# Last expert's first product with the slots held in the array and 256 weight columns streamed; layer 1's first expert picked by an early count; zero stores moved beside that expert

## The chip, the core and the metric

The kernel runs on one core of a Trainium2 chip. Time is device microseconds (us) of one execution; the figure that counts is the median of several. The core has a matrix engine (PE in the profile, its weight loads PEld), a vector engine (DVE), a scalar engine (ACT), GpSimd (POOL) and SP, which here only issues DMAs. Each of them runs its own instructions in order.

## What is computed

Retention attention over 2 batches of 8 heads, 768 positions and width 64, then two mixture-of-experts layers with 8 experts each: 1,536 tokens of 512 numbers, hidden width 1,024, one expert for each token. Layer 2 keeps at most 384 tokens for an expert.

```python
def _moe_ref(x, w_gate, w1, w2):
    logits = x @ w_gate
    expert_idx = np.argmax(logits, axis=1)
    ...
    gate_w = probs[np.arange(N), expert_idx]
    for e in range(E):
        mask = expert_idx == e
        xe = x[mask]
        h = np.maximum(xe @ w1[e], 0.0)
        ye = h @ w2[e]
        out[mask] = gate_w[mask, None] * ye

def reference(**kwargs):
    attn_out = _attn_ref(**attn_kwargs)
    x = attn_out.transpose(0, 2, 1, 3).reshape(B * S, H * D)
    x = _moe_ref(x=x, **moe_kwargs)
    return _moe2_ref(x=x, **moe2_kwargs)
```

With the inputs of the runs layer 1's experts get 183, 196, 188, 167, 213, 180, 203 and 206 tokens, in the order of their numbers (counted with the reference).

## The kernel before

**Attention** goes over 12 tiles of 128 tokens (the loop over `n`); each finished tile is stored to `x1d` in main memory by a DMA that ACT issues (`a_store`, L560), and routed: `batch` does that for several tiles at once (`BATCHES`: tiles 0 to 4, then 5 to 7), `route_tile` for the last four. In a batch, `pick` finds each token's expert, `count` (L593) adds tile by tile to the running counts `run`, `rank` and `slots` give each token its place, `place` (L619) makes the table of which token sits in which slot.

**Layers.** An expert has a fixed number of slots, `CAPS`: in layer 1 (`li == 0`) 220 for the first and 236, 220, 208, 200, 192, 184, 176 for the others, which follow by falling count (`finish_route` sorts them). Layer 1's first expert is always expert 0, so its weights are known from the start (`know(0, 0)`). Layer 2's first one is chosen while layer 1 still runs (`choose`, from the counts so far).

**The first expert** begins early. `early` gathers its first 128 slots from the first eight tiles (`eig`), and its first products run in full fp32 on whole weights (`products`, L429, two records for each product) while routing ends. The rest of its slots are gathered once all tiles are stored (`take` in `layer`, index `ig`, L344 on POOL), transposed in `first_x` (L370) and multiplied in the same way. `held` makes the first weight load of the next expert wait for that gather.

**The other experts** split every fp32 weight piece (512 KB, eight for each expert: four of the first product, then four of the second) into a high part by an ACT cast (`whi`, L163) and a low part by a subtraction (`wlo`, L174, on DVE, some on POOL). Weights are stationary and the slots move: high weights by high and low slots in one matmul (L788 or L814), low weights by high slots in a second (L789 or L815). SP loads pieces into four staging buffers `st` (L142), each free again when its `wlo` is done. `between(j, i)` stands after each eighth of expert `j` and issues the loads, splits, transposes and routing that run beside the products; `run_pend` does the same with what the expert before has left.

**Layer 2's last expert** has 128 slots. Its hidden part runs as for the others (`hidden_group`: 32 pairs of 256 and 128 moving columns, halves summed by ACT and DVE); its output part keeps the slots stationary and streams weights in two halves of 256 columns (`o_part`, L829 to L831), each scaled and scattered as soon as it is done.

**Zeros.** `x2d`, layer 1's output in main memory, is filled with zeros by 12 stores that SP issues behind the attention (L700), before layer 1 scatters its rows into it on POOL (`scatter`, L318).

Of the kernel before, what the change touches and what calls it, by code (L numbers as in the profile page):

```python
# [18 lines left out]
P = 128  # L19
# [8 lines left out]
CAPS = ((220, 236, 220, 208, 200, 192, 184, 176), (256, 256, 232, 208, 184, 168, 160, 128))  # L28
# [5 lines left out]
BATCHES = ((0, 5), (5, 8))  # L34
# [11 lines left out]
def _consts(capacity):  # L46
# [21 lines left out]
    put("first", np.broadcast_to(np.array([1e6] + [(E - e) / 16 for e in range(1, E)]), (P, E)))  # L68
# [5 lines left out]
    put("floor", np.broadcast_to(np.array([P] + [0] * (E - 1)), (P, E)))  # L74
# [7 lines left out]
def fused(ctx, tc, qT, kT, vkr, wg, w11, w12, w21, w22, cst, out, capacity):  # L82
# [41 lines left out]

    know(0, 0)
# [123 lines left out]
    def finish_route(rt, li, mix=()):  # L249
# [16 lines left out]
        V.tensor_add(key, nt, rt.get("first", con("first")))  # L266
# [96 lines left out]
    def first_x(rows):  # L363

        cnt = rows.shape[0]
        x = rp.tile([P, KD, P], F32, tag="x0", name="x0", bufs=2)[:, :, :cnt]
        for ks in range(0, 2), range(2, 4):
            tp = mmtile("tp").rearrange("p (k c) -> p k c", k=KD)[:, 0:2, :cnt]
            for i, k in enumerate(ks):
                T.transpose(tp[:, i, :], rows[:, k * P:(k + 1) * P], ident[:cnt, :cnt])  # L370
            A.copy(x[:, ks[0]:ks[-1] + 1], tp)
        return x


    def choose(rin, li):

        nt = mmtile("ch")[:, 0:E]
        T.matmul(nt, ones16, rin["S"], start=True, stop=True)
# [17 lines left out]
    def of_first(rin, a, dt, name):  # L396

        if "one" not in rin:
            return a[:, 0:1]
        junk = rp.tile([P, E], F32, tag="of", name="oj")  # L400
        f = rp.tile([P, 1], F32, tag="rmk", name="of")
        V.scalar_tensor_tensor(junk, a, 1.0, rin["one"], ALU.mult, ALU.mult, accum_out=f)
        if dt == F32:
            return f
        i = cp.tile([P, 1], dt, name=name)
        V.tensor_copy(i, f)
        return i

    def early(rin, xd, n):
# [4 lines left out]
        V.tensor_tensor(most, nt, rin.get("floor", con("floor")), ALU.max)  # L414
# [52 lines left out]
    with tc.tile_pool(name="ap", bufs=3) as ap:  # L467
# [180 lines left out]
        for n in range(NT):  # L648
            a_scores(n)
# [5 lines left out]
            if n:  # L655
                a_past(n - 1)
            if n == first + 2:
                many[0][2]()
            if n == second + 1:
                many[1][2]()  # L660
                many[1][3](3)
# [3 lines left out]
            if n == first + 1:  # L665
                many[0][1]()
            if n == first + 2:
                many[0][3](2)
            if n == first + 3:
                many[0][3](3)  # L670
# [28 lines left out]
        for t in range(NT):  # L699
            nc.sync.dma_start(x2d[t * P:(t + 1) * P, :], zero)  # L700
# [101 lines left out]

    def w2of(q0, f):
# [45 lines left out]
    def layer(li, xd, rin):  # L849
# [16 lines left out]
        def second():  # L866
            x[0] = first_x(rows[0][1])
            go(1)
# [30 lines left out]
        def between(j, i):  # L899
# [3 lines left out]
            if j + 2 == E and li == 0:  # L903
                if i == 0:
                    chosen.append(choose(rt[1], 1))
# [27 lines left out]

        for j in range(E):
# [6 lines left out]
            for i in range(4):  # L941
                if j == 0:
# [8 lines left out]
                    if i == 3:  # L951
                        between(0, i)
                else:
# [90 lines left out]
            elif j + 1 == E and cap == P:  # L1044
# [3 lines left out]
                for i2, lo in enumerate((0, D // 2)):  # L1048
                    p = mmtile("o")[:, 0:D // 2]
                    for i in range(4):  # L1050
                        o_part(q0, cap, h, [p], (2 * i, 2 * i + 1), 0, slice(lo, lo + D // 2))
                        if lo == 0:
                            between(j, 4 + i)
                    ob = xp.tile([P, D], F32, tag="ob", name="ob", bufs=2)[:, 0:D // 2]
                    A.activation(ob, p, AF.Copy, scale=gt[0])
# [315 lines left out]
```

## Time and profile before

| | |
|---|---|
| runs | 441.76, 442.85, 446.30 us; median 442.85 |
| profiled execution | 443.88 us; span of its instructions 442.1 us |
| granted PE clock, mean | 0.983 of full speed |
| busy | PE 411.3 us (93%), DVE 325.3 (74%), ACT 239.2 (54%), POOL 127.0 (29%) |
| DMA | 100.50 MB, mean 227 GB/s |

The span begins with the first instruction and ends with the last; 1.8 us of the execution lie outside. A "row" of the trace is a group of like instructions one behind the other: start, length, engine, line, operation, output and inputs, sizes, how many, and in brackets how long the engine sat idle before it and what ended that. Lengths of matmuls overlap, so the time that one takes of the engine is read from start to start.

### The profile page before, as it was taken

How to read it: one execution, taken by the hardware profiler on the slowest of the kernel's cores; microseconds unless marked ns; L12 is line 12 of the kernel's file. 1: busy time of each engine (PE TensorE's matmuls, PEld its weight loads, DVE VectorE, ACT ScalarE, POOL GpSimd, SP SyncE). 2: the span in 40 equal slices, each digit the busy share in tenths (PEclk: the TensorE clock that was granted, in tenths of full speed). 3: DMA queues.
4: the chain of work that ended last, by engine and by line, in shares of the span. 5: the costliest groups of instructions: out<-in, count | busy, mean ns of one | idle time of the engine just before them, and what ended most of it. 6: DMA issues, size and time to landing. Idle time of an engine off the chain costs nothing.

```text
span 442.1 us, 9412 instructions
## 1 busy us (share of the span) xinstructions
PE 411.3 (93%) x3373; PEld 384.4 (87%) x3373; DVE 325.3 (74%) x858; ACT 239.2 (54%) x493; POOL 127.0 (29%) x102
## 2 busy tenths in 40 slices
PE   8999884998999999999999999998999999999980
PEld 7887674998899999999989898997888999999970
DVE  3658896177989898989899877187586877887830
ACT  2111240266757666667666651366676777878730
POOL 2443113033353535344442204003202303201020
PEclk9999999799999999999999999999999999999996
DMA  8998994628575766666665733559758677777510
GB/s 317 391 310 300 380 387 148 215 97 264 189 257 169 240 212 241 215 234 220 231 218 191 266 128 89 231 191 313 271 184 269 221 261 249 256 245 247 188 43 14
DMA packets 32854, 100.50 MB, mean 227 GB/s; under 512 B 5008, under 2 KB 5520, under 8 KB 32800
## 3 DMA queue, kind: packets, MB, share of 16 engines
q1 hardware_dynamic: 25488, 82.75, 54.1%
q0 software_dynamic: 5008, 13.06, 8.8%
q10 hardware_dynamic: 2304, 4.02, 2.4%
q8 instruction: 28, 0.46, 0.4%
q14 instruction: 26, 0.21, 0.2%
HBM read 87.08 MB, written 13.05 MB: 226 GB/s over the span
## 4 chain that ended last, share of the span: by engine, by line
PE 59%; DVE 16%; DMA 10%; issue 9%; ACT 2%; POOL 1%; POOLq 0%; SPq 0%; ACTq 0%; DVEq 0%
PE y L814 14%; PE h L788 13%; PE y L815 6%; PE h L789 6%; DVE wlo L174 5%; PE h L429 4%; PE cb L1277 4%; DMA vk<-vkr 2%; DMA whole<-w 2%; DVE hs L774 2%; PE tp L359 2%; DVE h L800 2%; DMA rows<-x1d,eig 2%; DVE rkey L209 2%; PE o L829 1%
## 5 line engine op out<-in xcount | busy, mean ns | idle before, releaser
L174 DVE TENSOR_TENSOR wlo<-st,whi 128x1024 fp32r<-128x1024 f32 x107 | 141.2, 1328 | 0.9 <-ACT whi L163 0.9
L163 ACT CAST whi<-st 128x1024 fp32r<-128x1024 f32 x120 | 124.8, 1045 | 25.4 <-DMA st<-w 24.5
L788 PE MATMUL h<-x,whi 128*128 128x416 f32 (+10 forms) x416 | 123.5, 364 | 0.0
L814 PE MATMUL y<-h,whi 128*128 128x416 f32 (+8 forms) x384 | 117.6, 370 | 0.0
L789 PE MATMUL h<-x,wlo 128*128 128x208 f32 (+10 forms) x416 | 104.5, 251 | 0.0
L815 PE MATMUL y<-h,wlo 128*128 128x208 f32 (+8 forms) x384 | 97.3, 253 | 0.0
L788 PEld LDWEIGHTS h<-x,whi 128*128 128x128 f32 x416 | 78.1, 188 | 2.5 <-issue 0.4
L789 PEld LDWEIGHTS h<-x,wlo 128*128 128x128 f32 x416 | 79.5, 191 | 0.1
L814 PEld LDWEIGHTS y<-h,whi 128*128 128x128 f32 x384 | 72.1, 188 | 2.4 <-issue 0.2
L815 PEld LDWEIGHTS y<-h,wlo 128*128 128x128 f32 x384 | 73.4, 191 | 0.0
L174 POOL TENSOR_TENSOR wlo<-st,whi 128x1024 fp32r<-128x1024 f32 x13 | 34.9, 2684 | 57.7 <-ACT whi L163 51.3
L318 POOL DMA_INDIRECT out<-ob,is x14 | 13.9, 995 | 114.8 <-ACT ob L835 111.1
L800 DVE SCALAR_TENSOR_TENSOR h<-hs,h 128x416 fp32r<-128x416 f32 (+10 forms) x52 | 29.0, 558 | 20.7 <-ACT h L799 17.9
L799 ACT ACTIVATE h<-hs 128x416 fp32r<-128x416 f32 (+10 forms) x52 | 27.1, 521 | 31.1 <-DVE hs L774 30.5
L774 DVE TENSOR_TENSOR hs<-h,hb 128x208 f32<-128x208 f32 (+10 forms) x104 | 32.0, 347 | 6.5 <-ACT hb L773 4.8
L429 PE MATMUL h<-x,whole 128*128 128x128 f32 (+1 forms) x256 | 32.4, 288 | 0.0
L318 POOL DMA_INDIRECT x2d<-row,is x16 | 16.5, 1031 | 55.3 <-ACT row L1290 27.6
L429 PEld LDWEIGHTS h<-x,whole 128*128 128x128 f32 x256 | 31.3, 202 | 0.4 <-issue 0.2
L773 ACT COPY hb<-h 128x208 f32<-128x208 f32 (+10 forms) x104 | 28.8, 316 | 4.0 <-PE h L789 2.2
L1288 ACT COPY row<-cb 128x512 f32<-128x512 f32 x11 | 6.4, 585 | 38.9 <-DVE lgb L1283 29.2
L774 DVE TENSOR_TENSOR yt<-y,yb 128x220 f32<-128x220 f32 (+8 forms) x48 | 15.1, 355 | 14.7 <-ACT yb L773 14.7
L829 PE MATMUL o<-whi,h 128*128 128x512 f32 (+1 forms) x64 | 24.3, 380 | 0.0
(185 smaller groups left out, 604.8 us busy)
## 6 DMA issues: line engine op xcount, KB each, us to landing
st<-w SPq DMA_DIRECT2D x120, 512.0 KB, 4.2
vk<-vkr SPq DMA_DIRECT2D x11, 512.0 KB
whole<-w SPq DMA_DIRECT2D x8, 512.0 KB, 8.4
x2d<-zero SPq DMA_DIRECT2D x12, 260.0 KB, 5.8
qb<-qT SPq DMA_DIRECT2D x12, 256.0 KB, 6.8
x1d<-row ACTq DMA_DIRECT2D x11, 260.0 KB, 4.5
kt<-kT SPq DMA_DIRECT2D x11, 256.0 KB, 5.3
vk<-vkr ACTq DMA_DIRECT2D x1, 512.0 KB
```

Of the source, the lines that this page charges most:

```text
L163: A.copy(hi, st)
L174: (eng or V).tensor_sub(lo, st, hi)
L318: ins = nc.gpsimd.indirect_dma_start(dst.rearrange("n (i d) -> (n i) d", i=parts) if parts > 1 else dst[:, :], bass.IndirectOffsetOnAxis(a ...
L429: T.matmul(ps[:, j], w[:, k, j % 2 * P:(j % 2 + 1) * P], x[:, k], start=k == 0, stop=k == KD - 1, skip_group_check=True)
L773: A.copy(b, ps[:, 1, :])
L774: V.tensor_add(out, ps[:, 0, :], b)
L788: T.matmul(ps, hi[:, k, fs], x[:, k, :, :cap], start=k == 0, stop=False, skip_group_check=True)
L789: T.matmul(ps[:, 0, :], lo[:, k, fs], x[:, k, 0, :cap], start=False, stop=k == KD - 1, skip_group_check=True)
L800: V.scalar_tensor_tensor(h[:, sl, 1, :cap], s, 0.0, h[:, sl, 0, :cap], ALU.max, ALU.subtract)
L814: T.matmul(ps[i], hi[:, ds], h[:, f, :, :cap], start=f == 0, stop=False, skip_group_check=True)
L815: T.matmul(ps[i][:, 0, :], lo[:, ds], h[:, f, 0, :cap], start=False, stop=f == KF - 1, skip_group_check=True)
L829: T.matmul(p, h[:, f, 0, ts_], hi, start=f == 0, stop=False)
```

## The change

Four things are changed.

- Layer 1's first expert is no longer expert 0 but the one with the most tokens in the first four tiles. For that the batches become tiles 0 to 3 and 4 to 7 and their steps come about a tile earlier; `choose` is called at tile 7, and `know_first` reads the number on SP before the first weight loads at tile 8. `early` and the gather of the rest pick the chosen expert's column with `of_first` in place of column 0.
- `CAPS` of layer 1 become 240 for the first and 220, 208, 200, 192, 188, 184, 176.
- The 12 zero stores go from behind the attention into `between(0, i)` of layer 1, one or two for each `i`. `first_x` of layer 1's second gather gets 24 small matmuls on ones ahead of its transposes.
- In layer 2's last expert `hidden_rows` keeps the slots stationary and streams 256 weight columns; the result is rectified on ACT, turned by four transposes at a time and split again (`back_hidden`). The first four eighths of the output part are done for both halves ahead of the last four.

```diff
-CAPS = ((220, 236, 220, 208, 200, 192, 184, 176), (256, 256, 232, 208, 184, 168, 160, 128))
+CAPS = ((240, 220, 208, 200, 192, 188, 184, 176), (256, 256, 232, 208, 184, 168, 160, 128))
...
-BATCHES = ((0, 5), (5, 8))
+BATCHES = ((0, 4), (4, 8))
...
-    know(0, 0)
...
-        V.tensor_add(key, nt, rt.get("first", con("first")))
+        V.tensor_add(key, nt, rt["first"])
...
-    def first_x(rows):
+    def first_x(rows, warm=0):
...
-            tp = mmtile("tp").rearrange("p (k c) -> p k c", k=KD)[:, 0:2, :cnt]
+            tp = mmtile("tp")
+            for _ in range(0 if ks[0] else warm):
+                T.matmul(tp[:, 0:P], ones16, ones16, start=True, stop=True)
+            tp = tp.rearrange("p (k c) -> p k c", k=KD)[:, 0:2, :cnt]
...
         for n in range(NT):
+            if n == first + 1:
+                many[0][1]()
             a_scores(n)
...
+            if n == first + 1:
+                many[0][2]()
             if n == first + 2:
-                many[0][2]()
+                know_first = choose(rt1, 0, run[:, BATCHES[0][1], :])
             if n == second + 1:
                 many[1][2]()
-                many[1][3](3)
+                many[1][3](4)
...
             if n == NT - 4:
+                know_first()
                 refill(2)
...
-        for t in range(NT):
-            nc.sync.dma_start(x2d[t * P:(t + 1) * P, :], zero)
...
+    def hidden_rows(q0, x, i, ps):
+
+        hi, lo = (t.rearrange("p (k f) -> p k f", k=KD) for t in wq[q0 + i])
+        o = ps[:, i % 2 * 2 * P:(i % 2 + 1) * 2 * P]
+        for k in range(KD):
+            T.matmul(o, x[:, k, 0, :P], hi[:, k, :], start=k == 0, stop=False, skip_group_check=True)
+            T.matmul(o, x[:, k, 0, :P], lo[:, k, :], start=False, stop=False, skip_group_check=True)
+            T.matmul(o, x[:, k, 1, :P], hi[:, k, :], start=False, stop=k == KD - 1, skip_group_check=True)
+
+    def back_hidden(hr, h, b):
+
+        tp = mmtile("th").rearrange("p (f c) -> p f c", f=4)
+        for f in range(4):
+            T.transpose(tp[:, f, :], hr[:, f * P:(f + 1) * P], ident)
+        sl = slice(4 * b, 4 * b + 4)
+        A.copy(h[:, sl, 0, :P], tp)
+        V.tensor_sub(h[:, sl, 1, :P], tp, h[:, sl, 0, :P])
...
-            x[0] = first_x(rows[0][1])
+            x[0] = first_x(rows[0][1], 24)
...
             refill()
+            if li == 0 and j == 0:
+                for t in range(NT * i // 8, NT * (i + 1) // 8):
+                    nc.sync.dma_start(x2d[t * P:(t + 1) * P, :], zero)
...
+                elif rows_first(j):
+                    if i % 2 == 0:
+                        ps = mmtile("hr")
+                    hidden_rows(q0, x[j], i, ps)
+                    run_pend()
+                    if i == 2:
+                        back_hidden(hr, h, 0)
+                    if i % 2:
+                        hr = xp.tile([P, 2, C0], F32, tag="hs", name="hr", bufs=2).rearrange("p a c -> p (a c)")
+                        A.activation(hr, ps, AF.Relu)
+                    between(j, i)
...
+                some(0, (0, 1))
+                back_hidden(hr, h, 1)
+                some(0, (2, 3))
+                some(1, range(4))
+                for i in range(4):
+                    between(j, 4 + i)
+                for i2 in range(2):
+                    some(i2, range(4, KF))
```

SP, from the last weight loads of the attention on, before (`order_1179` is the sorted list of experts that SP reads a number from, `whole` the first expert's weights, `st` a staged piece):

```order
L142 DMA st<-w 128x1024 x2
L154 DMA whole<-w 128x1024 x4
L142 DMA st<-w 128x1024 x2
L700 DMA x2d<-zero 128x520 x12
L283 TENSOR_LOAD order_1179
L283 ISA x2
L902 TENSOR_LOAD order_1179
L902 ISA x2
L142 ISA
L142 DMA st<-w 128x1024
```

And after, from that reading of the list on (`order_1204`):

```order
L917 TENSOR_LOAD order_1204
L917 ISA x2
L138 ISA
L138 DMA st<-w 128x1024
L138 ISA
L138 DMA st<-w 128x1024
L926 DMA x2d<-zero 128x520
L138 ISA
L138 DMA st<-w 128x1024
L138 ISA
L138 DMA st<-w 128x1024
L926 DMA x2d<-zero 128x520 x5
```

The twelve stores have left the place behind the attention; the first stands behind two loads of layer 1's second expert, five more behind the next two, and the last six, not shown, one or two at a time between the eight loads that follow.

DVE, in the attention at tile 7, before (`run` are the counts, `Am` and `xt` belong to the attention itself):

```order
L506 TENSOR_TENSOR Am<-sc,cs 128x4x128 x2
L1283 TENSOR_REDUCE lgb<-cb 128x8
L523 TENSOR_TENSOR wn_626<-du,wm_489 128x256
L593 TENSOR_TENSOR run<-run,boh 128x8 x5
L553 TENSOR_TENSOR xt<-ot,cs 128x256 x2
L506 TENSOR_TENSOR Am<-sc,cs 128x4x128 x2
```

And after, at the same tile (`ck` to `floor` are `choose`; `bR` are the slots of a tile's tokens):

```order
L504 TENSOR_TENSOR Am<-sc,cs 128x4x128 x2
L1323 TENSOR_REDUCE lgb<-cb 128x8
L380 TENSOR_TENSOR ck<-ch,cs 128x8
L382 TENSOR_REDUCE cm<-ck 128x1
L384 TENSOR_SCALAR one_638<-ck,cm 128x8
L387 SCALAR_TENSOR_TENSOR cj,ce<-one_638,cs 128x8
L389 CAST chosen_643<-ce 128x1
L391 SCALAR_TENSOR_TENSOR first_645<-one_638,cs 128x8
L393 TENSOR_SCALAR floor_647<-one_638 128x8
L521 TENSOR_TENSOR wn_658<-du,wm_489 128x256
L609 TENSOR_SCALAR bR<-iota_79,r_123 128x256 x2
L551 TENSOR_TENSOR xt<-ot,cs 128x256 x2
```

Counts stood there before; now seven operations of `choose` and two of `slots` stand ahead of the tile's `xt`.

PE, at the end of the hidden part of layer 2's last expert and the start of its output part, before:

```order
L788 MATMUL h<-x,whi 128x256
L789 MATMUL h<-x,wlo 128x128
L829 MATMUL o<-whi,h 128x256
L830 MATMUL o<-wlo,h 128x256
L831 MATMUL o<-whi,h 128x256
```

And after (`hr` are the hidden rows, slot by slot, `th` their transposes):

```order
L805 MATMUL hr<-whi,x 128x256
L806 MATMUL hr<-wlo,x 128x256
L807 MATMUL hr<-whi,x 128x256
L844 MATMUL o<-whi,h 128x256
L845 MATMUL o<-wlo,h 128x256
L846 MATMUL o<-whi,h 128x256
L844 MATMUL o<-whi,h 128x256
L845 MATMUL o<-wlo,h 128x256
L846 MATMUL o<-whi,h 128x256
L813 MATMUL th<-cs,hr 128x128 x4
L844 MATMUL o<-whi,h 128x256
```

Three products of 256 weight columns stand where two of 256 and 128 slot columns stood, and the second set of transposes stands behind six products of the output part.

## Rows read from the trace of the kernel before

**Rows 1.** Page, chain that ended last, shares of the span by engine.
```profile
PE 59%; DVE 16%; DMA 10%; issue 9%; ACT 2%; POOL 1%; POOLq 0%; SPq 0%; ACTq 0%; DVEq 0%
```

**Rows 2.** Windows, one expert each: bounds, length, busy time by engine, clock, DMA.
```profile
98.90:125.40 26.50, 24.73 (x163) 22.23 (x162) 23.09 (x57) 17.06 (x34) 11.73 (x7) 1.00 0.65 214
125.40:148.50 23.10, 23.10 (x163) 22.01 (x162) 20.77 (x53) 15.65 (x32) 10.13 (x7) 1.00 0.65 221
148.50:171.00 22.50, 22.50 (x162) 21.94 (x161) 20.15 (x52) 15.36 (x32) 10.09 (x7) 1.00 0.67 225
171.00:193.60 22.60, 22.24 (x162) 21.61 (x161) 20.30 (x55) 15.19 (x32) 10.28 (x7) 1.00 0.65 224
193.60:215.80 22.20, 21.83 (x163) 21.22 (x162) 19.94 (x54) 15.02 (x32) 10.20 (x7) 1.00 0.67 226
215.80:239.20 23.40, 22.35 (x164) 21.09 (x163) 21.02 (x64) 14.87 (x32) 9.30 (x6) 1.00 0.61 213
...
338.10:358.40 20.30, 20.30 (x137) 19.89 (x136) 14.38 (x25) 13.95 (x29) 6.85 (x6) 1.00 0.75 244
...
396.90:414.70 17.80, 17.80 (x142) 17.77 (x141) 14.97 (x30) 13.43 (x31) 1.96 (x2) 1.00 0.73 247
```

**Rows 3.** Timeline of PE, the transposes of layer 1's second gather.
```profile
77.47 0.84 PE L370 MATMUL tp<-cs,rows 92*128 92x92 f32 x4 [5.79 <-DMA rows<-x1d,ig]
```

**Rows 4.** Timeline of POOL, that gather's issue.
```profile
72.13 1.25 POOL L344 DMA_INDIRECT rows<-x1d,ig  x1 [15.64 <-DVE z L303]
```

**Rows 5.** Zero stores, 40 to 90 us: instructions, first and last start, landing times.
```profile
L700 SPq DMA_DIRECT2D x2d<-zero x12: 319/320/745, 52.5 to 66.5; - x12
...
DMA to landing us min/median/max: 5.3/5.8/7.0
```

**Rows 6.** Tile stores to x1d, 40 to 90 us: instructions, first and last start.
```profile
L560 ACTq DMA_DIRECT2D x1d<-row x7: 326/327/345, 41.2 to 66.1; - x7
```

**Rows 7.** Tile stores to x1d, 0 to 40 us: landing times.
```profile
DMA to landing us min/median/max: 3.6/4.2/5.4
```

**Rows 8.** Windows of 2 us around that wait, columns as in rows 2.
```profile
74.00:76.00 2.00, 0.00 (x0) 0.00 (x0) 0.79 (x1) 0.00 (x0) 1.70 (x2) 0.82 0.28 65
...
80.00:82.00 2.00, 2.00 (x12) 2.00 (x10) 0.69 (x1) 0.60 (x1) 0.00 (x0) 0.50 0.83 250
...
84.00:86.00 2.00, 2.00 (x20) 2.00 (x20) 0.67 (x3) 0.64 (x2) 0.00 (x0) 1.00 0.66 264
```

**Rows 9.** Window, products L429 of 128 slots alone (PE, PEld, clock, DMA).
```profile
67.00:71.80 4.80, 4.68 (x41) 4.49 (x40) 1.00 0.60 201
```

**Rows 10.** Windows of the attention at tiles 6 and 10, columns as in rows 2.
```profile
28.35:32.65 4.30, 4.30 (x74) 3.70 (x72) 2.56 (x8) 0.68 (x2) 1.65 (x3) 1.00 0.85 258
...
47.56:53.46 5.90, 4.43 (x67) 3.66 (x65) 5.33 (x20) 1.28 (x2) 1.04 (x1) 1.00 1.01 389
```

**Rows 11.** Timeline of DVE, counting of a batch.
```profile
37.16 1.38 DVE L593 TENSOR_TENSOR run<-run,boh 128x8 f16<-128x8 f16 x5
```

**Rows 12.** Timeline of PE in layer 2's last expert.
```profile
418.81 0.60 PE L1040 MATMUL o<-cs,yt 128*32 128x128 f32 x4
419.16 0.36 PE L788 MATMUL h<-x,whi 128*128 128x256 f32 x1
...
422.90 0.33 PE L829 MATMUL o<-whi,h 128*128 128x256 f32 x1
423.08 0.28 PE L830 MATMUL o<-wlo,h 128*128 128x256 f32 x1
...
425.08 0.36 PE L829 MATMUL o<-whi,h 128*128 128x256 f32 x1
```

**Rows 13.** Timeline of ACT, a cast that waits for its piece.
```profile
99.74 1.06 ACT L163 CAST whi<-st 128x1024 fp32r<-128x1024 f32 x1 [1.74 <-DMA st<-w]
```

**Rows 14.** Loads of weight pieces, 93 to 108 us: instructions, first and last start.
```profile
L142 SPq DMA_DIRECT2D st<-w x6: 333/333/642, 93.8 to 104.7; - x6
```

**Rows 15.** Timeline of DVE, the index of layer 1's second gather.
```profile
67.12 0.17 DVE L242 TENSOR_TENSOR ig<-tbp,tb 128x16 int32<-128x16 f32 x1 [0.53 <-PE cnt L245]
```

More of the change, by code (lines that the diff above doesn't have):

```diff
@@ L67, in _consts @@
     put("tok", P * np.arange(NT)[None, :] + s[:, None])
-    put("first", np.broadcast_to(np.array([1e6] + [(E - e) / 16 for e in range(1, E)]), (P, E)))
     put("tie", np.broadcast_to((E - np.arange(E)) / 16, (P, E)))
@@ L73, in _consts @@
     put("held", np.broadcast_to(np.array(CAPS[1]), (P, E)))
-    put("floor", np.broadcast_to(np.array([P] + [0] * (E - 1)), (P, E)))
     cand = np.arange(P) // NM
@@ L372, in first_x, with choose @@
         return x
-    def choose(rin, li):
+    def choose(rin, li, S):
         nt = mmtile("ch")[:, 0:E]
-        T.matmul(nt, ones16, rin["S"], start=True, stop=True)
+        T.matmul(nt, ones16, S, start=True, stop=True)
         key = rp.tile([P, E], F32, tag="ju", name="ck")
@@ L396, in of_first @@
     def of_first(rin, a, dt, name):
-        if "one" not in rin:
-            return a[:, 0:1]
         junk = rp.tile([P, E], F32, tag="of", name="oj")
@@ L413, in early @@
         most = rp.tile([P, E], F32, tag="ju", name="most")
-        V.tensor_tensor(most, nt, rin.get("floor", con("floor")), ALU.max)
+        V.tensor_tensor(most, nt, rin["floor"], ALU.max)
         V.tensor_scalar(rin["S"], most, ident[:, 0:1], None, ALU.mult)
@@ L664, in fused @@
                 many[0][0]()
-            if n == first + 1:
-                many[0][1]()
-            if n == first + 2:
+            if first < n < first + 3:
                 many[0][3](2)
-            if n == first + 3:
-                many[0][3](3)
             if n == second:
@@ L904, in between @@
                 if i == 0:
-                    chosen.append(choose(rt[1], 1))
+                    chosen.append(choose(rt[1], 1, rt[1]["S"]))
                 if i == 2:
@@ L932, in between, with rows_first @@
                 gate[j + 1] = gate[j + 1][1]()
+        def rows_first(j):
+            return li == 1 and j + 1 == E and caps[j] == P
         for j in range(E):
@@ L1047, in layer, with some @@
                     V.tensor_scalar(ix2[:, i:i + 1], ix["isc"][:, j:j + 1], 2.0, float(i), ALU.mult, ALU.add)
[L1048 to L1053, printed above, removed]
+                ps = [mmtile("o")[:, 0:D // 2] for _ in range(2)]
+                def some(i2, fs):
+                    o_part(q0, cap, h, [ps[i2]], fs, 0, slice(i2 * D // 2, (i2 + 1) * D // 2))
+                some(0, (0, 1))
[6 more added lines that the diff above has]
+                    some(i2, range(4, KF))
                     ob = xp.tile([P, D], F32, tag="ob", name="ob", bufs=2)[:, 0:D // 2]
-                    A.activation(ob, p, AF.Copy, scale=gt[0])
+                    A.activation(ob, ps[i2], AF.Copy, scale=gt[0])
                     scatter(out, ix2[:, i2:i2 + 1], ob)
```

## The prediction

> **What bounds the kernel now.** I read the chain that ended last first: PE holds 59% of it, DVE 16%, DMAs 10% [rows 1]. So most of what is saved on PE should come out at the end, and a DMA or a vector step counts only at a few places. The windows by expert say which places. From 125 us on PE is busy for the whole of a layer 1 window or within 0.4 us of it, up to the expert of 184 slots, where 1.05 us are missing [rows 2]. DVE is busy for some 20 us of each, so it stands close behind. The clear hole comes earlier: before the transposes of layer 1's second gather PE sat idle for 5.79 us, until that gather's DMA had landed [rows 3]. PE had stopped at 77.47 - 5.79 = 71.68. The gather was issued only at 72.13 [rows 4], though its index was begun at 67.12 [rows 15]; it landed at 77.47. What held it back is not named in the row, whose releaser had long been done. It has to wait for the last tile stores to `x1d`, which began at 66.1 [rows 6]. Beside them ran the twelve zero stores, begun from 52.5 to 66.5, which took 5.3 to 7.0 us to land [rows 5]; the last of these landed at about 72, when the gather went. The hole costs twice: the granted clock was 0.82 in 74 to 76, PE having done nothing since 71.68, and 0.50 in 80 to 82; it is 1.00 again in 84 to 86, after products at the half rate (1.2 in place of 2.4 GHz) [rows 8].
>
> **Zero stores and the second gather.** The stores leave this stretch, so the last tile store, of 128 columns and the logits, has the DMA engines almost to itself. Its price alone is not in the trace. The nearest rows are tile stores at 0 to 40 us, of twice the size and beside busy engines: 3.6 us at the least [rows 7]. I take 3.0; the ends are 3.6 and the time at which the index is there. The Trainium skill's page "DMA: Bandwidth & Descriptors" (Anatomy of one DMA) gives 2.0 us and the bytes at 436 GB/s; by that the store would land in an estimated 2.3 us and the sum be 0.7 us lower. The store's issue shifts by what the attention gains or loses. `choose` adds seven small operations on DVE, `of_first` two to four ahead of each gather, and a tile moves from the first batch to the second. The nearest row is a count, 1.38 us for five such operations, 0.28 each [rows 11]: some 2 us of DVE for the seven, or 0 if they fall into its gaps. At tile 6 a tile takes 4.30 us with DVE busy for 2.56, but at tile 10 it takes 5.90 with DVE at 5.33 [rows 10]; the new ones stand at tile 7, where about half can be covered. I take 0.8 us later, from 0 to 2. The last store is then issued at 66.1 + 0.8 = 66.9 and lands at 69.9, and the gather goes 72.13 - 69.9 = **2.2 us** sooner. At best, with the index (67.12 + 0.17 [rows 15]) and 0.8 for two more operations and the attention, it is at 68.1, 4.0 sooner; at worst 0.5. The gather's own 5.3 us until PE starts stay, since DMA was nearly idle in 74 to 76 already, 65 GB/s [rows 8].
>
> **Clock.** PE now ends its early products at about 71.68 + 0.8 = 72.5 and then runs the 24 small matmuls: at no more than the 0.114 us of a product record (4.68 us for 41 [rows 9]) 2.7 us, at half of that 1.4. They end at 73.9 to 75.2, the rows are there at 75.3. The idle time is at most 1.4 us against 5.79, so I expect a clock of 1.00 throughout. What the half clock cost: 12 records in 2 us in 80 to 82, 0.167 each, against 20 in 2 us, 0.100, in 84 to 86 [rows 8]. From 78.0 to 82.2 stood 8 records of 128 slots (0.21 against 0.114: 0.8 us) and some 14 of 92 (0.067 each: 0.9 us); the four transposes took 0.84 us [rows 3] against 0.60 for four at the full clock [rows 12]. Together **1.9 us** less.
>
> **Slots.** The first expert's second part grows from 92 to 112 slots. A record takes 0.100 us at 92 and 0.114 at 128, so about 0.108 at 112; 64 records cost **0.5 us** more. For the experts that follow, two bounds. Layer 2's windows for 208 and 160 slots are 20.30 and 17.80 us [rows 2]: 0.052 us for each slot. The seven experts lose 1,416 - 1,368 = 48 slots, 2.5 us at that price. Layer 1's own windows give less: 26.5 for 236 slots falls by 16 x 0.052 = 0.8 to 220; then 23.1 for 220, 22.5 for 208, 22.6 for 200 and 22.2 for 192 are each replaced by the next, and 192 by 188 changes nothing, since at 184 the window was longer again, 23.4 [rows 2], and what is late there is DVE's routing. That is 0.8 + 0.6 - 0.1 + 0.4 = 1.7; I take **1.8 us** less, with 1.0 and 2.5 as ends. The first expert's output part has 20 slots more for half an expert's work: 10 x 0.052 = **0.5 us** more.
>
> **Where the zero stores go.** Six stand among the first four loads of layer 1's second expert, six among the eight that follow, on SP's queue and so behind every wait of a load. The first six are harmless: the four loads now land while the first expert's fp32 products run, and no cast asks for a piece before the output part. The other six lie beside loads that ACT waits for: one cast waited 1.74 us for its piece [rows 13]. But those six loads were issued over 11 us, 93.8 to 104.7 [rows 14], so there are gaps. I take **0.3 us** more, from 0 to 1.5. The last two come behind the sixth of these loads, so they would land at about 104.7 + 0.7 + 5.3 = 110.7 in the old count. Layer 1's first scatter on POOL waits for all twelve, and behind it the next scatter, a subtraction and two gathers; POOL is busy for 11.73 of the 26.50 us of that window [rows 2] and can catch up, so I charge nothing, and up to 1 us of the 1.5 if the subtracted piece is needed at once.
>
> The Trainium skill speaks against this move: "DMA: Bandwidth & Descriptors" (Queues, rings and completion order) says that the semaphore of a transfer rises only after every earlier write of that DMA engine, across its queues. By it the zero stores did hold the `x1d` stores back, as the landing times suggest, but now each piece behind a zero store would be reported no sooner than that store; that is the third rival below.
>
> **The last expert.** The 32 pairs of 256 and 128 columns follow each other at (422.90 - 419.16)/16 = 0.234 us, 7.5 us in all. Products of 256 weight columns on stationary slots exist already, in the output part: 17 of them from 423.08 to 425.08, 0.118 each [rows 12]. The 48 new ones take 5.65 us, 1.8 less. Two sets of four transposes come in, each (419.16 - 418.81) = 0.35 us [rows 12], 0.7 together. The second set waits for ACT's rectified rows; six products, 0.7 us, cover that. A cast of twice the columns took 1.06 us [rows 13], so the wait is at most some 0.4 us; I take 0.2. ACT's copy and DVE's subtraction behind it have 18 products, 2.1 us, as cover. At the end half an output of 12 products in place of 24 lies between the two scatters, which changes only when the first goes. And DVE and ACT lose the sums of halves, which nobody waited for here. 1.8 - 0.7 - 0.2 and a little from the output part, whose old order waited for its last slots: **1.2 us** less, from 0.4 to 1.5.
>
> **Sum.** -2.2 - 1.9 + 0.5 - 1.8 + 0.5 + 0.3 - 1.2 = -5.8 us. Against the profiled execution, 443.88 us, that is 438.1; this one lay 1.0 us over the median of the three runs, and from 442.85 it is 437.05. I predict **437.0 us**, 1.3% less.
>
> **Rivals.**
> *The gather goes no sooner*, because something other than the zero stores sets 72.13, for instance the wait of POOL for another DMA that I can't see. For it: no row names the releaser. Against it: the landing times fit. Then the idle time behind the small matmuls is still over 2 us, the clock may fall again, and 2.2 + 1.9 are lost: 437.0 + 4.1 = 441.1. Chance 0.16.
> *Everything pays in full*: the gather 4.0, slots 2.5, tail 1.5, no price for the moved stores: -4.0 - 1.9 + 1.0 - 2.5 - 1.5 = -8.9, 434.0. For it: PE is dense in nearly every window. Chance 0.14.
> *The zero stores only change place* (the slower end). All twelve, 12 x 260 KB = 3.1 MB, stand on the same queue as the second expert's pieces; at the 389 GB/s of the fullest window [rows 10] they are 8 us of transfer, and where ACT already waits for a piece [rows 13] each is added to that wait, and ACT's next sums of halves hold PE's banks. Then 437.0 + 8 = 445. It turns the sign if over 5.8 of the 8 us come out on PE, which asks that the stores land in front of needed loads rather than between them; six of them don't. Chance 0.06.
> *The tail doesn't do what it says*: the chain transposes, ACT, DVE, product shows in full and eats the 1.2 us: 438.2. Against it: products of other slices stand between. Chance 0.10.
> The forecast has the remaining 0.54.
>
> **How the numbers follow.** Three runs spread from 441.76 to 446.3 us; under about 1% no difference can be told from none. 1% below the median is 438.4. The forecast lies below that with some 4 in 5 (0.43), the full payment always (0.14), the tail's failure half (0.05), and a part of the first rival: faster 0.64. Slower by over 1% (447.3) needs the third rival and more: 0.04. Within 1%: 0.32. The range reaches from 433.6, just under the full payment, to 441.3, just over the first rival; it leaves out the third rival and the far ends of the terms, less than 2 in 10.
>
> **What would show it.** After: the gather's idle time in front of the transposes near 1 us in place of 5.79, issued near 70; a clock of 1.00 from 70 to 90; L429's records of 112 slots near 0.108; the layer 1 windows some 0.4 us shorter up to 192 slots; DMA below 100 GB/s at 64 to 68 us; the last expert's products at 0.118 and its hidden part near 6.5 us. The prediction is wrong if the gather still goes at 72, if ACT's waits for pieces grow by microseconds between 85 and 105, if the attention is over 2 us longer, or if layer 1's windows stay at their old lengths because DVE, not PE, sets them.

## The result, and the profile after

The changed kernel takes 438.94 us, median of 14 runs (436.96 to 441.69), against 444.72 us for the kernel before in 14 runs beside them (441.76 to 452.22). The ratio is 0.989, 95% interval 0.987 to 0.992. (The kernel before is sometimes disturbed, with a lower clock; the ratio leaves those runs out, so it is closer to one than the medians are.) 437.0 us, 1.3% less, was predicted; 1.1% less was measured. The profiled execution took 440.08 us with a span of 438.3, against 442.1 before: 3.8 us, while the ratio gives some 4.8. Behind the end of PE's products lie some 13 us of span in both.

The total hides that the parts came out otherwise. First the stretch of the second gather; timeline of the changed kernel, from ACT, DVE, POOL and PE:

```profile
65.42 0.33 ACTq L558 DMA_DIRECT2D x1d<-row  x1
...
67.69 0.15 DVE L404 CAST ig<-of 128x1 int32<-128x1 f32 x1
...
68.65 1.00 POOL L340 DMA_INDIRECT rows<-x1d,ig  x1 [12.45 <-DVE at L268]
...
71.62 1.50 PE L367 MATMUL tp<-ones 128*128 128x128 f16 x24
72.96 0.56 PE L370 MATMUL tp<-cs,rows 112*128 112x112 f32 x4
...
81.32 0.46 PE L829 MATMUL y<-h,whi 128*128 128x480 f32 x1
```

What the DMA view says of that last tile store (KB, us from issue to landing):

```profile
x1d<-row ACTq DMA_DIRECT2D x1, 132.0 KB, 1.9
```

The gather leaves 3.23 us behind the issue of the last tile store, in place of 6.0 us [rows 4, 6]. The store has landed by 67.3, the last step of the gather's index ends at 67.84, and the gather follows that by 0.81 us: now the index sets it, no longer the store. PE goes from the early products through the small matmuls to the transposes without a wait, where it had idled 5.79 us [rows 3]. The windows of 2 us of the changed kernel, for PE alone (length, PE busy and records, granted clock, DMA share, GB/s), show the clock there, against 0.82 and 0.50 in [rows 8], and two windows in which it falls now:

```profile
74.00:76.00 2.00, 2.00 (x20) 1.00 0.98 346
...
80.00:82.00 2.00, 2.00 (x18) 1.00 0.98 372
...
114.00:116.00 2.00, 2.00 (x11) 0.66 0.75 270
116.00:118.00 2.00, 2.00 (x10) 0.50 0.69 254
```

The first expert's output part begins at 81.32 in place of 88.01. But of these 6.7 us the second expert gives 3.8 back. The windows by expert, columns as in [rows 2]:

```profile
92.70:123.00 30.30, 25.55 (x163) 23.64 (x162) 21.98 (x57) 18.51 (x39) 10.36 (x7) 0.94 0.75 254
123.00:145.30 22.30, 22.30 (x162) 21.96 (x161) 20.30 (x50) 14.92 (x28) 9.50 (x7) 1.00 0.59 204
...
411.10:425.10 14.00, 13.84 (x114) 13.09 (x112) 5.79 (x13) 7.69 (x14) 3.44 (x3) 1.00 0.22 78
```

The second expert has 16 slots fewer and takes 30.3 us in place of 26.5, at a clock of 0.94; the third, with 208 slots in place of 220, takes 22.3 in place of 23.1. Where the second one loses shows in the timeline of ACT, POOL and DVE:

```profile
92.90 1.05 ACT L159 CAST whi<-st 128x1024 fp32r<-128x1024 f32 x1 [3.87 <-DMA st<-w]
94.81 1.05 ACT L159 CAST whi<-st 128x1024 fp32r<-128x1024 f32 x1 [0.87 <-DMA st<-w]
...
108.33 1.04 POOL L314 DMA_INDIRECT x2d<-row,is  x1 [13.05 <-DMA st<-w]
109.67 0.98 POOL L314 DMA_INDIRECT x2d<-row,is  x1 [0.30 <-ACT whi L159]
110.66 2.38 POOL L170 TENSOR_TENSOR wlo<-st,whi 128x1024 fp32r<-128x1024 f32 x1
...
110.51 2.56 DVE L221 TENSOR_SCALAR E<-roh,tk 128x8 f16<-128x8 f16 x1
112.99 0.15 DVE L222 TENSOR_TENSOR S<-S,roh 128x8 f16<-128x8 f16 x1
```

and in the waits of PE from 80 to 126 us (total, times, longest):

```profile
PE rk L218 <- DVE S L222: 2.3, 1, 2.3
PE cb L1317 <- DVE yt L771: 1.3, 1, 1.3
PE cb L1317 <- ACT row L1330: 1.2, 1, 1.2
```

The last two zero stores begin at 100.2 and 100.7, and POOL's first scatter to `x2d`, whose rows are ready at 101.6, goes only at 108.33. (By the profile the store begun at 100.7 lands 6.2 us later, at 106.9; what fills the 1.4 us from there it doesn't show. Its releaser, a piece's load, is only what ended last before.) POOL's subtraction, queued behind both scatters, begins at 110.66, and beside it DVE takes 2.56 us for a product of 8 columns. The count `S` waits for that, PE's rank product waits for `S`, and after these 2.3 us without work the granted clock is 0.66 and then 0.50, which is 1.2 in place of 2.4 GHz. The casts' waits of 3.87 and 0.87 us come earlier, in the first expert's output part and just behind it.

### The profile page after: what moved, and what is told of

The parts are those of the page before. It is cut to its first block, busy times and chain, and to the rows that moved or that the text cites. A ratio compares the mean times of both kernels' runs of the same rounds, so it can differ in the third digit from the quotient of the medians.

```text
span 438.3 us, 9454 instructions
## 1 busy us (share of the span) xinstructions
PE 409.2 (93%) x3390; PEld 382.3 (87%) x3390; DVE 323.1 (74%) x863; ACT 238.5 (54%) x485; POOL 126.8 (29%) x102
## 4 chain that ended last, share of the span: by engine, by line
PE 54%; DVE 18%; issue 10%; DMA 9%; ACT 3%; POOL 1%; SPq 1%; POOLq 0%; ACTq 0%; DVEq 0%
PE y L829 13%; PE h L785 11%; DVE wlo L170 6%; PE y L830 5%; PE h L786 5%; DMA st<-w 5%; PE h L427 4%; DMA vk<-vkr 3%; PE cb L1317 3%; DVE hs L771 2%; DVE h L797 2%; DVE rkey L205 2%; PE tp L355 2%; PE o L844 1%; PE o L846 1%
## 5 line engine op out<-in xcount | busy, mean ns | idle before, releaser
L829 PE MATMUL y<-h,whi 128*128 128x416 f32 (+9 forms) x384 | 117.9, 372 | 0.0
L785 PE MATMUL h<-x,whi 128*128 128x416 f32 (+9 forms) x384 | 114.5, 365 | 0.0
L830 PE MATMUL y<-h,wlo 128*128 128x208 f32 (+9 forms) x384 | 97.4, 254 | 0.0
L786 PE MATMUL h<-x,wlo 128*128 128x208 f32 (+9 forms) x384 | 96.7, 252 | 0.0
L786 PEld LDWEIGHTS h<-x,wlo 128*128 128x128 f32 x384 | 73.3, 191 | 0.1
L797 DVE SCALAR_TENSOR_TENSOR h<-hs,h 128x416 fp32r<-128x416 f32 (+9 forms) x48 | 27.0, 562 | 18.8 <-ACT h L796 18.3
L796 ACT ACTIVATE h<-hs 128x416 fp32r<-128x416 f32 (+9 forms) x48 | 25.1, 523 | 27.1 <-DVE hs L771 27.0
L771 DVE TENSOR_TENSOR hs<-h,hb 128x208 f32<-128x208 f32 (+9 forms) x96 | 29.7, 348 | 7.0 <-ACT hb L770 6.9
L770 ACT COPY hb<-h 128x208 f32<-128x208 f32 (+9 forms) x96 | 26.9, 318 | 4.2 <-PE h L786 4.0
L771 DVE TENSOR_TENSOR yt<-y,yb 128x208 f32<-128x208 f32 (+9 forms) x48 | 15.1, 353 | 18.0 <-ACT yb L770 18.0
```

What stands on the lines that cost most here:

```text
L770: A.copy(b, ps[:, 1, :])
L771: V.tensor_add(out, ps[:, 0, :], b)
L785: T.matmul(ps, hi[:, k, fs], x[:, k, :, :cap], start=k == 0, stop=False, skip_group_check=True)
L786: T.matmul(ps[:, 0, :], lo[:, k, fs], x[:, k, 0, :cap], start=False, stop=k == KD - 1, skip_group_check=True)
L797: V.scalar_tensor_tensor(h[:, sl, 1, :cap], s, 0.0, h[:, sl, 0, :cap], ALU.max, ALU.subtract)
L829: T.matmul(ps[i], hi[:, ds], h[:, f, :, :cap], start=f == 0, stop=False, skip_group_check=True)
```

## The experiments

All of them start from the changed kernel.

**Zero stores back behind the attention.**

```
+        for t in range(NT):
+            nc.sync.dma_start(x2d[t * P:(t + 1) * P, :], zero)
...
-            if li == 0 and j == 0:
-                for t in range(NT * i // 8, NT * (i + 1) // 8):
-                    nc.sync.dma_start(x2d[t * P:(t + 1) * P, :], zero)
```

> The changed kernel with the twelve zero stores back in their old place on SP, behind the attention's loads; all else as changed. Theory: they had held layer 1's second gather (issued at 72.13 before, 68.65 after), and at their new place they cost the second expert 4 to 5 us. Then the gather goes at about 72 again and the first expert's output part, at 81.32 after, starts 3 to 4.5 us later; but the casts' waits for pieces in the second expert (3.87 and 0.87 us after) are gone, and the third expert starts at 122 to 123, as it does after (122.99): the two moves cancel, about 439 us in all. Rival 1: the early choice set the gather's time, not the stores. Then the gather stays near 68.7, the output part near 81.3, and the third expert starts near 119: 435 us. Rival 2: the second expert's loss has nothing to do with the stores. Then the output part comes late and nothing is won back: third expert at 126 to 127, 442 to 443 us.

Measured: 439.83 us (6 runs), ratio to the kernel before 0.990 (0.987 to 0.993). The timeline of POOL and PE:

```profile
73.82 1.86 POOL L340 DMA_INDIRECT rows<-x1d,ig  x1 [16.43 <-DVE over L304]
...
78.10 0.64 PE L370 MATMUL tp<-cs,rows 112*128 112x112 f32 x4 [3.93 <-DMA rows<-x1d,ig]
```

A window of 2 us behind it, for PE alone:

```profile
80.00:82.00 2.00, 2.00 (x12) 0.51 0.96 306
```

The window of the second expert, all engines:

```profile
99.60:125.10 25.50, 23.59 (x162) 22.04 (x161) 22.16 (x56) 16.64 (x33) 10.91 (x7) 1.00 0.68 220
```

What the DMA view says of the last tile store here:

```profile
x1d<-row ACTq DMA_DIRECT2D x1, 132.0 KB, 5.4
```

The gather is late again (6.2 us behind the last tile store, issued at 67.62, which takes 5.4 us to land in place of 1.9), PE idles 3.93 us in spite of the small matmuls, and the clock falls as before. So the zero stores did hold the gather, by way of the tile store, and the early choice is not what freed it. The second expert, though, takes 25.5 us, its hidden part 13.41 and its output part 12.14, against 15.02 and 15.24 in the changed kernel. The theory holds in kind: one move wins 6.8 us ahead of the first output part (88.14 in place of 81.32, of which 1.2 lie in this execution's attention) and loses 4.7 in the second expert. Its sizes were off: it had 3 to 4.5 us for the output part and the third expert at 122 to 123, which starts at 125.12, and of the casts' waits, which it had gone, one of 2.33 us is left. Since the second expert also starts 6.8 us later here, this run alone does not tell the stores' share of the 4.7 us from that of the earlier start; the next two runs do for the output part.

**All twelve stores in one run behind the fourth load.**

```
-            if li == 0 and j == 0:
-                for t in range(NT * i // 8, NT * (i + 1) // 8):
+            if li == 0 and j == 0 and i == 1:
+                for t in range(NT):
```

> The changed kernel with all twelve zero stores in one run behind the first four loads of the second expert's pieces (from about 76 us), none among the later loads. SP sat without an issue from 79.8 to 87.2 after, so there is room. Theory: the six late stores (87.6 to 101) made the pieces late (cast waits of 3.87 and 0.87 us), kept POOL's first scatter until 108.3 and set its late subtraction beside DVE's routing (2.56 us for one small operation). Then gather and output part stay as after (68.7 and 81.3), the casts' waits fall under 1.5 us together, the first scatter goes before 104, and the third expert starts at 119 to 120 in place of 122.99: 435 to 436 us, 0.980 of the kernel before. Rival: the second expert is short of cover because it starts 6 us earlier while its pieces have only four buffers and are loaded when these come free; then the third expert still starts at 122 to 123 and the time stays at 439.

Measured: 437.59 us (433.64 to 437.9, 5 runs), ratio 0.983 (0.979 to 0.988). Timeline of ACT, POOL, DVE and PE:

```profile
94.37 1.05 ACT L159 CAST whi<-st 128x1024 fp32r<-128x1024 f32 x1 [3.73 <-DMA st<-w]
...
102.74 1.03 POOL L314 DMA_INDIRECT x2d<-row,is  x1 [5.85 <-ACT row L1330]
...
107.53 3.03 POOL L170 TENSOR_TENSOR wlo<-st,whi 128x1024 fp32r<-128x1024 f32 x1 [0.15 <-ACT whi L159]
...
108.99 1.59 DVE L205 SCALAR_TENSOR_TENSOR rkey<-row,rm,cs 112x8 f32<-112x8 f32 x1
...
112.13 0.22 DVE L221 TENSOR_SCALAR E<-roh,tk 128x8 f16<-128x8 f16 x1
...
112.47 0.21 PE L218 MATMUL rk<-S,ones 128*112 128x8 f16 x1 [0.74 <-DVE S L222]
```

The second expert's window:

```profile
94.30:120.70 26.40, 23.96 (x163) 22.16 (x161) 22.26 (x57) 17.69 (x34) 10.76 (x7) 1.00 0.66 219
```

The scatter goes as soon as its rows are there, PE's rank product waits 0.74 us in place of 2.26, the output part takes 12.16 us with a clock of 1.00, and the third expert starts at 120.70 although this execution's first output part began 1.6 us later (82.92). The output part's 3.1 us are thus the late stores' doing. The subtraction on POOL has not stopped disturbing DVE: now it is the key `rkey` that takes 1.59 us, in place of 0.23 (in the kernel before it took 1.55). Nobody on PE's path waits for that one. The casts' wait, however, did not fall (3.73 us), the hidden part still takes 14.23 us, and the time lies 1.6 us above the upper end of the theory: here the rival has a share.

**One of POOL's subtractions given to DVE, the late stores left.**

```
-POOL = (((1, 5),) * (E - 1) + ((),), ((),) * E)
+POOL = (((1, 5), (5,)) + ((1, 5),) * (E - 3) + ((),), ((),) * E)
```

> The changed kernel with one of the second expert's two subtractions on POOL, the one at 110.66, given to DVE (1.22 us there); the zero stores stay among the later loads, POOL's first scatter still waits for the last of them until about 108. Theory: the loss of 3.1 us in the second expert's output part (15.24 us, against 12.16 where the stores were early) is the overlap of that subtraction with DVE's one-hot product (2.56 us in place of 0.22), which keeps PE 2.26 us at the rank product and then lowers its clock to 0.50. Then that operation takes 0.22 us again, PE waits at most 1.2 us (DVE's extra 1.22 us stands ahead of it), the clock stays near 1.00 and the output part takes 12.2 to 13.5 us: 436 to 437.5 us. Rival: the late scatter or the late stores hold PE themselves, POOL's subtraction is only beside it; then the output part stays at 15 us and the time at 439.

Measured: 437.37 us (436.43 to 438.8, 6 runs), ratio 0.985 (0.981 to 0.990). Timeline of POOL and DVE:

```profile
111.45 2.55 POOL L314 DMA_INDIRECT x2d<-row,is  x1 [12.96 <-DVE roh L212]
...
113.60 0.39 DVE L221 TENSOR_SCALAR E<-roh,tk 128x8 f16<-128x8 f16 x1
```

A window for PE alone, where the clock had fallen:

```profile
114.00:116.00 2.00, 1.93 (x13) 1.00 0.87 57
```

The second expert's window:

```profile
95.90:122.30 26.40, 23.96 (x163) 22.16 (x161) 22.23 (x55) 16.87 (x33) 8.98 (x6) 1.00 0.82 265
```

The first scatter is as late as ever, yet the product takes 0.39 us, PE waits 0.8 us at the rank product, the clock stays 1.00 and the output part takes 12.25 us. Late stores and a late scatter alone cost PE nothing there; what costs is the subtraction beside DVE's routing.

**Six and six stores.**

```
-            if li == 0 and j == 0:
-                for t in range(NT * i // 8, NT * (i + 1) // 8):
+            if li == 0 and j == 0 and i < 2:
+                for t in range(6 * i, 6 * i + 6):
```

> The changed kernel with six zero stores behind the first two loads of the second expert (from 73 us) and six behind the next two (from about 77). With all twelve behind the fourth load, the next piece, issued at 88.8 into a full DMA (1.06 busy from 84 to 90), still landed after 5.5 us and a cast waited 3.73 us for it; the second expert's hidden part took 14.23 us, against 13.41 with the stores in the attention. Theory: four microseconds earlier they are through by 87, that wait falls to 2 us or less and the hidden part to 13.4 to 13.8: 0.4 to 0.8 us under the kernel with all twelve behind the fourth load, 436.5 to 437.3 us. Rival: now the third and fourth piece land behind six stores, the casts at 86 to 89 wait for them instead, and nothing is won: 437.6 us or up to 1 us more.

Measured: 436.99 us (436.7 to 438.97, 6 runs), ratio 0.985 (0.980 to 0.990). The hidden part takes 13.43 us and the longest wait of a cast is 2.38 us, as the theory had it; but the expert also starts 1.2 us later here (95.48), so this does not show that the stores' place did it. The 0.6 us on the median are within the spread.

**Fewer small matmuls.** Without them, in the changed kernel (`first_x(rows[0][1], 24)` becomes `first_x(rows[0][1], 0)`):

> The changed kernel without the 24 small matmuls ahead of the second gather's transposes. Theory: with the gather at 68.65 PE idles only some 1.3 us from 71.6, and the matmuls merely fill that time. If an idle stretch of 1.3 us lowers the clock, the granted clock falls under 1.00 between 73 and 82 and the output part starts 0.5 to 1.9 us later than 81.32 (the 1.9 us is what the half clock cost before, behind 5.79 us of idle time): 439.5 to 441 us. If not, the clock stays 1.00, the output part starts within 0.2 us of 81.32 and the time is that of after, 439: the whole of the clock's gain then comes from the earlier gather.

Measured: 441.19 us (438.77 to 444.76, 12 runs), ratio 0.995 (0.992 to 0.998): slower than the changed kernel, though the two intervals just touch. Neither branch of the expectation has this time: the first needs a lower clock, and the profiled execution shows no loss in this place. PE's timeline:

```profile
72.92 0.57 PE L370 MATMUL tp<-cs,rows 112*128 112x112 f32 x4 [0.30 <-DMA rows<-x1d,ig]
```

A window behind it:

```profile
74.00:76.00 2.00, 2.00 (x20) 1.00 0.96 302
```

PE waits 0.30 us, the clock stays 1.00, and the time from the early products to the output part is 15.84 us, 1.0 less than with the 24. Nor do the other runs look like a lower clock: their mean granted clock is 0.982 to 0.990, against 0.981 to 0.987 in the changed kernel, and the slowest, 444.76 us, has 0.984 where the fastest has 0.985. A second profile of the same kernel:

> The changed kernel without the 24 small matmuls once more, for a second profile: the first profiled execution, 438.77 us, was the fastest of twelve whose median is 441.19. Theory: in a usual execution PE idles long enough ahead of the transposes that the granted clock falls below 1.00 between 73 and 83, and the output part starts 1 to 2 us later against the early products' start than the 15.84 us of the first profile. Rival: the clock stays 1.00 there, and the 2 us of the median are lost elsewhere (the attention, the end, or a later wait).

One run, 439.60 us: a wait of 0.32 us, a clock of 1.00 from 74 to 84, 16.05 us to the output part, and in the second expert the rank wait of 2.5 us and the low clock as in the changed kernel. The rival is what this profile shows, but it does not show where a run of 441 or more loses its time. With the stores early, 8 matmuls, and then none:

> The kernel with all twelve zero stores behind the fourth load, and 8 small matmuls in place of 24 ahead of the second gather's transposes. Theory: the rows are there before the 24 are through (they ran from 73.21 to 74.55 and the transposes followed without a wait), so 16 fewer of 0.056 us each start the transposes up to 0.9 us sooner, with a clock of 1.00: 436.7 to 437.3 us. Rival: with the matmuls left out altogether the time was 2 us longer though the profiled execution showed no lower clock in this stretch; if they serve something else, 8 are too few and the time is 438 to 440 us.

> The kernel with all twelve zero stores behind the fourth load, without any small matmul ahead of the transposes. With 24 of them its median was 437.59, with 8 it was 436.96. Theory: the matmuls are not needed once the gather goes at 69 to 70 us, since in both profiles without them PE waited only 0.3 us for the rows and the granted clock stayed 1.00; then the time is 436.5 to 437.5 us and the 441.19 of the changed kernel without them was chance of those twelve runs. Rival: they guard against executions in which the rows come later, which the two profiles happened not to show; then the time is 439 us or more here too, with a wider spread.

8 gave 436.96 us (436.16 to 437.51, 6 runs), ratio 0.984 (0.979 to 0.988); none gave 437.64 (436.42 to 438.81, 6 runs), 0.984 (0.980 to 0.988). The number makes no difference that can be measured there. That the matmuls guard against late rows is not borne out; why the changed kernel without them has the median of 441.19 stays open.

**Both small edits together**, six and six stores with 8 matmuls:

> The two edits that each gave some 0.6 us beside the twelve early stores, together: six zero stores behind the first two loads of the second expert and six behind the next two, and 8 small matmuls ahead of the transposes. Theory: they act at different places (the second expert's hidden part 13.43 in place of 14.23 us, and up to 0.9 us ahead of the transposes), so they add: 436.0 to 436.6 us, 0.982 of the kernel before. Rival: a sooner start of the second expert only lengthens its casts' waits for pieces, and the two do not add: 437 us.

Measured: 437.76 us (436.68 to 438.36, 6 runs), ratio 0.985 (0.981 to 0.989): they don't add. The second expert starts at 92.01, 3.5 us sooner than with the six and six stores alone (0.9 of it from the 16 matmuls; in the other profile the early products also ran in part at a clock of 0.50), but its hidden part takes 15.25 us in place of 13.43. The rival's mechanism is what this profile shows.

**The last expert as before.** Its two parts in the form of the kernel before, all else as changed (`rows_first` returns `False`, and the output loop is the old one):

> The changed kernel with the last expert computed as before: weights stationary in the first products, the sums of halves, no transposes, one output half after the other. By the prediction the new form is worth 1.2 us, so this would be 440.1 us. By the two traces it is worth 8.19 + 6.19 - 7.57 - 6.47 = 0.34 us, so 439.3 us, and the last expert's two parts take 14.4 us in place of 14.0. Everything up to the start of the last expert stays as after (411.1 +- 0.5).

Measured: 438.31 us (437.37 to 439.95, 6 runs), ratio 0.988 (0.985 to 0.992): the same as the changed kernel, and below both sums of the expectation. By its window the new form is worth 0.6 us (14.60 against 14.00), against the kernel before 0.3:

```profile
410.40:425.00 14.60, 14.57 (x122) 13.98 (x120) 7.70 (x23) 8.26 (x22) 2.89 (x3) 1.00 0.27 92
```

## Why the prediction came out right, and where it did not

The time lies in the range and the sign is right, but two errors of more than 3 us each, in opposite senses, nearly cancel: the way to the first output part (the first three rows below) gained 6.7 us where 3.6 were forecast, and the zero stores' new place cost 4.7 where 0.3 were. That the total came out so near is luck. From the profiled executions:

| step | predicted | measured |
|---|---|---|
| gather sooner | -2.2 | -3.5 (72.13 to 68.65) |
| from its issue to the transposes | 0 | -1.0 (5.34 to 4.31) |
| clock, and 112 slots | -1.4 | -2.2 (transposes to output part, 10.54 to 8.36) |
| first expert's output part | +0.5 | +0.5 (10.92 to 11.41) |
| zero stores' new place | +0.3 | +4.7 with what comes from the earlier start |
| later experts of layer 1 | -1.8 | -1.9 (-0.9 and -1.0) |
| layer 2 up to the last expert | 0 | -0.3 |
| last expert | -1.2 | -0.3 (14.38 to 14.04) |

With the 0.1 us by which the end behind PE grew this gives, but for rounding, the 3.8 us of the two spans.

**Gather.** What held it before was read rightly, as the run with the stores back shows. What sets it afterwards was not. The forecast let the gather wait for the last tile store, at a price of 3.0 us, and had the index only as its best end. But the store (132 KB: 256 columns and the logits, not 128) lands 1.9 to 2.2 us after its issue, in the seven profiles that have its landing. The Trainium skill's page "DMA: Bandwidth & Descriptors" (Anatomy of one DMA) had given an estimate of 2.3, from a fit for transfers that GpSimd issues; this one goes from ACT's queue, and the rows lie nearer to that than to 3.0. In all ten profiles with the stores moved the gather begins 0.81 or 0.82 us behind the last step of its index (L404 on DVE), while its distance from the store's issue varies from 3.2 to 4.2. The size is in part chance: over these ten profiles the gather is issued between 68.65 and 70.90, with a median of 69.9. That is the forecast's own figure, reached by a wrong cause, and the changed kernel's profile is the earliest of the ten. And the gather's own 5.3 us were kept, on the ground that DMA was nearly idle then; the rows are there within 3.4 to 3.5 us in the three profiles where PE has no matmuls to finish (69.48 to 72.92 in one). Why it took 5.34 in the kernel before is not shown.

**Clock.** It stays 1.00, as forecast. The stretch from the transposes on gained 2.2 us where 1.4 were forecast: the half clock had cost more than the 1.9 us charged. In the profiles the small matmuls are not what keeps the clock: without them it stays as well (three profiles), and with them it falls to 0.51 when the rows come 3.93 us late.

**Zero stores.** This is the step that failed: "I take 0.3 us more, from 0 to 1.5". It looked for the price at ACT's pieces, whose waits between 85 and 105 us grew only from 3.6 to 4.7 in all, and at POOL it said that POOL "can catch up, so I charge nothing, and up to 1 us of the 1.5 if the subtracted piece is needed at once". The piece was not what was needed. POOL caught up by running its subtraction later, and there it shut DVE out of an operation on PE's path: 1.5 us more of waiting (2.26 in place of 0.74) and some 1.6 us of low clock behind it, 3.1 us of the output part. This is shown twice, by early stores with the subtraction kept, and by late stores without the subtraction. The third rival had the right sign and the wrong place: transfers in front of pieces.

The other 1.6 us, in the hidden part, are not shown to be the late stores' at all. In the five profiles with late stores the hidden part takes 13.8 to 15.0 us, over starts from 92.7 to 95.9, and 14.2 and 15.0 in two that start at 92.73. In the five kernels with early stores it takes 13.4 to 15.3 us, longest where it starts first, and the output part begins at 107.3 to 109.0 in all of them, over starts from 92.0 to 95.5. The pieces have four buffers, and each load is issued when DVE or POOL has emptied one; ACT waits 2.4 to 4.4 us for the fifth piece in each. I read from this that the early start outruns the pieces, which no term had; a run with more buffers was not made.

**Later experts.** The term, 1.8 us between its two bounds, was right, the second expert's share measured in the run with the stores back (25.55 us against 26.43), the others' in the changed kernel.

**Last expert.** The products take 0.118 us as forecast, yet the hidden part takes 7.57 us where 6.5 were forecast. What was mis-sized is what interrupts the products. The previous expert's transposes now fall among products that are over sooner (0.85 us with a wait of 0.16 for DVE, and 0.36; before 0.36 and 0.35), and the first product after each set takes 0.08 us longer. The two own sets cost 0.40 and 0.55, the second waiting for the rectified rows, about the 0.9 charged. No measurement of the whole kernel separates the two forms. The tail rival was nearer than the forecast in size, but not in its reason: the chain in which it saw the price cost what was charged.

The better kernels: with early stores, whatever the number of matmuls, or with the one subtraction moved, all medians lie between 436.96 and 437.76, 1.2 to 2.0 us under the changed kernel, and in each of their profiles the collision is gone. Among them the measurement can't choose, and the intervals of their ratios still touch that of the changed kernel; it is the profiles that tell them from it. From the start of the early products to the end of PE's products, which leaves out the attention and the end, these six take 357.2 to 358.5 us; the four profiles with the collision (the changed kernel, that without matmuls twice, the old last expert) take 359.8 to 360.7.

## What to carry to other kernels

When a transfer is moved, follow its completion as well as its issue: who waits for the last of them, what stands behind that one in its queue, and what runs beside those instructions at the new time. A delay on an engine that "can catch up" is free only if its late work meets nobody on the critical path. And a gain that starts one stage sooner is kept only as far as the next stage's inputs come sooner too; here the next expert's hidden part took 13.43 us or 15.25, longer where it started 3.5 us sooner, which I put down to its four weight buffers without having tried more.

## What the hardware showed that was not expected

A DVE operation on 8 columns, 0.22 us by itself, took 2.56 us beside a POOL subtraction of 2.38 us and ended with it (113.07 and 113.04); in three other profiles with this overlap it took 2.54 to 2.71, and where another small operation met the subtraction that one took 1.59 in place of 0.23. The Trainium skill's page "SBUF — State Buffer" (Who interferes with whom) says that the two engines share one pair of ports as an exclusive lock, which an instruction that needs it holds for its whole length while the other engine's waits, and that whoever issues first gets it. The key's row agrees: it begins behind the subtraction (108.99 against 107.53) and ends with it (110.58 and 110.56). The product's rows agree in length but not plainly in order: in all four profiles it begins 0.13 to 0.28 us ahead of the subtraction, while the scatter before that still runs on POOL, and loses all the same; why is not shown.

From the issue of the last scatter to the end of the span pass 10.4 to 12.3 us over the twelve profiles (425.75 to 436.1 with the last expert as before, 425.97 to 438.3 in the changed kernel), with no work left on any engine that would explain the difference. The attention's end varies by another 2.5 us (early products between 64.4 and 66.9 us in the kernels that share it). One profiled execution against another is therefore good to 2 us or more in its span. Some parts between repeat to 0.1 (the first expert's output part 11.39 to 11.43 us in the eleven profiles with 240 slots), others do not: the second expert's hidden part differs by 0.4 us between two profiles without the matmuls (14.20 and 13.79).
